# Where the last weights of a two-matrix feed-forward layer are converted: during attention, or beside the second pass

## The chip, the core and the metric

One NeuronCore of a Trainium2 chip runs the whole program in one launch. The metric is device time in microseconds (us), the median of several executions. PE is TensorE (matmul), DVE is VectorE, ACT is ScalarE, POOL is GpSimd, and SP is the engine whose queue issues nearly all DMA transfers here. Every engine executes its own instructions strictly in the order in which the build left them, and waits at an instruction until what it needs has happened.

## The reference, cut to what matters

```python
# q, k, v: (8 batches, 8 heads, 576 positions, 64)
scores = scale * q @ k.T                      # causal in blocks of 64 positions
attn = softmax(where(block_i >= block_j, scores, -1e9))
x = (attn @ v).transpose(0, 2, 1, 3).reshape(4608, 512)
out = ((x @ w_a) * (x @ w_b)) @ w_out         # w_a, w_b: 512 x 1536, w_out: 1536 x 512
```

The three weight matrices reach the kernel as 64-bit floating-point numbers, so they have to be turned into 32-bit numbers on the chip before TensorE can use them. This conversion is what the case is about.

## The kernel before, in words

**Blocks.** The 1536 hidden columns are 12 blocks of 128, numbered f = 0 to 11. A block needs its part of w_a and w_b (tensor `wab`, in two halves i = 0, 1 of 512 values a partition) and its rows of w_out (tensor `wo`, one piece of 512 values a partition). Every matmul is made of three: the operands are split into a high part that TensorE takes exactly (type fp32r) and a low rest, and high x high, high x low and low x high are added.

**Conversion of one piece** (`fetch`, `convert`, `sums`, `split`; L122 to L178). A DMA brings 512 KB into `raww`. Then come: DVE L139 (exponent out of the upper word, `sw`), ACT L140 (scaled exponent), DVE L143 and L145 (mantissa, `mw`), DVE L147 (sign and exponent together, `sw`) and DVE L149 (the 32-bit number, `xw`). A piece of `wo` is then split: ACT L110 writes the high part, DVE or POOL L113 the low one. A half of `wab` of the blocks 4 to 11 needs seven combinations instead of four (see the second pass): four small DVE sums (L172), two copies on ACT (L165, L175) and two subtractions on DVE (L177, L178). `convert` and `sums` are generators: each `next` is one step, and the steps are put between other work. With `paced`, a step's DVE instruction may not stand ahead of a named earlier instruction (`behind_of`).

**Attention** (64 heads, a slot of the loop at L598 for each). In a slot TensorE makes scores of one head (`sl`, `s`, L394, L414), turns the softmax result of the head before (`tp`, L467) and multiplies earlier ones with v (`av`, L516 to L522). DVE finds maxima (`nm`, L400), sums and the reciprocal of the sums (`rc`, L434 to L441); ACT makes exponentials (L403); POOL multiplies them by `rc` (`e`, L444); TensorE turns `e`; ACT copies it out of PSUM as high part (`ah`, L469) and DVE subtracts the low part (`al`, L471). Every second slot DVE also splits q of a pair of heads (`qp`, L341). SP copies q and k within the chip (`q<-qp`, `k<-kp`, L360, L361) two slots ahead of their use, through single buffers.

**First pass.** During attention the blocks 0 to 3 are applied to the tokens that are done (`ab_unit`, `o_unit`, `mm3`, L217), a fixed share of matmuls in each slot, and fill TensorE. Partial results go to DRAM (`part`). The product of a and b is `hf` (DVE, L243). The weights of these four blocks are converted in the first slots.

**Second pass** (L797 to L851). It covers six tiles of 768 tokens with the blocks 4 to 7 (`ps_` = 0), then the same six tiles with the blocks 8 to 11 (`ps_` = 1). For each block `pair_unit` makes seven products instead of eight (`psy`, `psx`, `psw`, `psv`, L705) that DVE combines (`u_z`, L723 to L733); POOL and ACT split the results (`h_z`), and `pair_out` (`pso_z`, L751) adds the four blocks. x is read back from DRAM (`xr`), and DVE, ACT and POOL form and split its combinations for the next tile (`sums_x`, L668).

**Where the blocks 4 to 11 are converted before the change.** The eight `wab` halves of the blocks 4 to 7 are converted while the first pass ends; their four `wo` pieces in the first tile. The weights of the blocks 8 to 11 (eight `wab` halves, four `wo` pieces) are converted during the tiles 1 to 4, one step for every 10 matmuls (`STEP2` = 1600), into a buffer `st`, and stored in DRAM (`wabd`, `wod`). In tile 5 they are loaded for the second sweep. The order of instructions within an engine is set at the build by a scheduler, in whose program order the steps stand where `next` is called.

## Time and profile before

| what | us |
|---|---|
| median of three runs (lowest, highest) | 1290.13 (1284.51, 1292.95) |
| the profiled execution, its own time | 1293.99 |
| its span, first to last instruction | 1292.2 |
| PE busy, share of the span | 1242.7, 96% |
| DVE busy, share of the span | 1000.4, 77% |
| ACT busy, share of the span | 686.9, 53% |
| POOL busy, share of the span | 545.0, 42% |

In a table of stretches each row gives the stretch, its length, then the busy time and number of instructions of PE, PEld (weight loads), DVE, ACT and POOL, the granted TensorE clock as a share of full speed, the busy share of the DMA engines and their GB/s. A stretch in which PE is busy for its whole length can get shorter only by fewer matmuls; where PE has idle time, the question is on whom it waited.

### The profile page before, as it was taken

Reading aid. Unit: us, or ns where it says so; the run is one execution under the profiler, and the core shown is the slowest. Engines: PE = TensorE matmul, PEld = TensorE weight load, DVE = VectorE, ACT = ScalarE, POOL = GpSimd, SP = SyncE. Lnnn points to the kernel's source line nnn. Section 1 sums busy time; section 2 is a strip of 40 time slices with the busy share of each in tenths; the row PEclk is TensorE's granted clock in tenths of the full one; section 3 lists DMA queues with packets and bytes.
Section 4 is the critical chain, followed back from the end, with each engine's and each line's share of the span. In section 5 each row is a group of like instructions: output and inputs, shape, how many; then the busy total and the mean of one; then the engine's idle time right before and its main releaser. Section 6 shows DMA issues by size and latency. Waiting matters only on the chain.

```text
span 1292.2 us, 23401 instructions
## 1 busy us (share of the span) xinstructions
PE 1242.7 (96%) x7849; PEld 1177.4 (91%) x7849; DVE 1000.4 (77%) x2325; ACT 686.9 (53%) x1722; POOL 545.0 (42%) x681
## 2 busy tenths in 40 slices
PE   9998999999999999999998998999999899999998
PEld 5677989999999999999997998999999899999998
DVE  6877778778878787887789999899976576577563
ACT  5787777788787887887745423233322222222210
POOL 4667555555565555655522223223123123123231
PEclk8999999999999999999998999999999899999999
DMA  5466667766676666677224355464466442242131
GB/s 194 138 188 169 170 170 180 176 166 171 165 182 171 168 178 164 163 187 172 82 93 149 111 190 163 163 195 157 159 205 238 160 148 65 83 147 87 61 98 62
DMA packets 93496, 196.58 MB, mean 152 GB/s; under 512 B 11968, under 2 KB 52928, under 8 KB 93376
## 3 DMA queue, kind: packets, MB, share of 16 engines
q1 hardware_dynamic: 88768, 185.64, 50.8%
q10 hardware_dynamic: 4608, 9.44, 2.0%
q8 instruction: 63, 1.03, 0.3%
q14 instruction: 57, 0.47, 0.1%
HBM read 96.47 MB, written 47.19 MB: 111 GB/s over the span
## 4 chain that ended last, share of the span: by engine, by line
PE 61%; DVE 21%; issue 6%; DMA 5%; ACT 4%; POOL 2%; SPq 0%; ACTq 0%; DVEq 0%; POOLq 0%
PE pso_z L751 13%; PE ps L217 8%; PE psx_z L705 6%; PE psw_z L705 6%; PE psv_z L705 6%; PE tp L467 5%; DVE al L471 3%; PE s L394 3%; PE pso L217 3%; DVE nm L400 3%; PE psy_z L705 3%; PE av L522 2%; PE av L506 2%; POOL e L444 2%; DMA kp<-kT 1%
## 5 line engine op out<-in xcount | busy, mean ns | idle before, releaser
L113 POOL TENSOR_TENSOR h_z<-u_z,h_z 128x384 fp32r<-128x384 f32 x96 | 112.9, 1176 | 400.8 <-ACT h_z L110 378.2
L217 PE MATMUL ps<-xh,wab 128*128 128x288 f32 x1024 | 245.9, 306 | 0.0
L444 POOL TENSOR_SCALAR e<-e,rc 128x512 f32<-128x512 f32 (+3 forms) x256 | 152.3, 608 | 154.6 <-DVE rc L441 148.1
L751 PE MATMUL pso_z<-h_z,wo 128*128 128x384 f32 x1152 | 203.8, 335 | 3.5 <-POOL h_z L113 3.5
L751 PEld LDWEIGHTS pso_z<-h_z,wo 128*128 128x128 f32 x1152 | 199.6, 188 | 5.8 <-POOL h_z L113 5.8
L471 DVE TENSOR_TENSOR al<-tp,ah 128x512 fp32r<-128x512 f32 x224 | 138.8, 620 | 63.7 <-ACT ah L469 61.6
L217 PEld LDWEIGHTS ps<-xh,wab 128*128 128x128 f32 x1024 | 173.7, 190 | 3.6
L467 PE MATMUL tp<-ident,e 128*128 128x128 f32 x832 | 136.3, 279 | 18.5 <-POOL e L444 11.6
L217 PE MATMUL ps<-xl,wab 128*128 128x288 f32 x512 | 152.8, 299 | 0.2 <-POOL xl L113 0.2
L110 ACT CAST h_z<-u_z 128x384 fp32r<-128x384 f32 x96 | 49.4, 514 | 167.2 <-DVE u_z L730 162.1
L469 ACT CAST ah<-tp 128x512 fp32r<-128x512 f32 x224 | 119.2, 534 | 35.0 <-PE tp L467 33.3
L467 PEld LDWEIGHTS tp<-ident,e 128*128 128x128 f32 x832 | 99.3, 142 | 36.2 <-POOL e L444 21.4
L217 PE MATMUL pso<-hh,wo 128*128 128x288 f32 x512 | 128.5, 312 | 3.2 <-ACT hh L110 3.2
L705 PE MATMUL psx_z<-xh,wab 128*128 128x384 f32 x384 | 118.5, 344 | 9.0 <-DVE u_z L723 8.6
L403 ACT ACTIVATE e<-s,nm 128x192 f32<-128x192 f32 (+2 forms) x192 | 101.8, 531 | 36.7 <-DVE nm L400 30.1
L705 PE MATMUL psw_z<-xh,wab 128*128 128x384 f32 x384 | 117.3, 341 | 0.8 <-DVE u_z L725 0.8
L705 PE MATMUL psv_z<-xh,wab 128*128 128x384 f32 x384 | 117.2, 340 | 0.5 <-DVE u_z L727 0.4
L400 DVE TENSOR_REDUCE nm<-s 128x1 f32<-128x128 f32 (+3 forms) x256 | 110.2, 432 | 4.4
L217 PEld LDWEIGHTS ps<-xl,wab 128*128 128x128 f32 x512 | 97.3, 190 | 3.9 <-POOL xl L113 0.4
L217 PEld LDWEIGHTS pso<-hh,wo 128*128 128x128 f32 x512 | 89.2, 193 | 5.3 <-ACT hh L110 3.9
L113 POOL TENSOR_TENSOR v<-vr,v 128x320 fp32r<-128x320 f32 x56 | 49.4, 883 | 85.6 <-ACT v L110 63.7
L394 PE MATMUL s<-k,q 128*128 128x256 f32 x336 | 81.7, 325 | 2.6 <-ACT e L403 1.4
(143 smaller groups left out, 2913.3 us busy)
## 6 DMA issues: line engine op xcount, KB each, us to landing
k<-kp SPq DMA_DIRECT2D x112, 288.0 KB, 4.0
xr<-xd SPq DMA_DIRECT2D x48, 384.0 KB, 3.5
pt<-part SPq DMA_DIRECT2D x96, 192.0 KB, 3.5
q<-qp SPq DMA_DIRECT2D x112, 160.0 KB, 2.8
raww<-wab SPq DMA_DIRECT2D x24, 512.0 KB, 3.8
qp<-qT SPq DMA_DIRECT2D x32, 320.0 KB, 3.1
vr<-vm SPq DMA_DIRECT2D x64, 160.0 KB, 3.4
kp<-kT SPq DMA_DIRECT2D x32, 288.0 KB, 3.1
```

The source lines that it names most:

```text
L110: nc.scalar.copy(hi, src)
L113: return lo_eng.tensor_tensor(lo, src, f32(hi), op=ALU.subtract)
L217: mm = nc.tensor.matmul(ps, w_, d_, start=(i == 0), stop=(i == n - 1))
L394: mark = nc.tensor.matmul(ps[:, :w], qm[:, q0[t]:q0[t] + P], kk[:, :w], start=(i == 0), stop=(i == len(ks) - 1))
L400: nc.vector.tensor_reduce(nm[:, t:t + 1], view, axis=AX.X, op=ALU.max, negate=True)
L403: nc.scalar.activation(out, view, AF.Exp, bias=bias, accum_out=sm[:, t, :1])
L444: nc.gpsimd.tensor_scalar(ev, ev, rc[:, t:t + 1], 1.0, op0=ALU.mult, op1=ALU.mult)
L467: mark = nc.tensor.transpose(tp[:, c], src, ident)
L469: nc.scalar.copy(ah[:, :m, cols], tp[:, :m])
L471: return nc.vector.tensor_tensor(al[:, :m, cols], tp[:, :m], f32(ah[:, :m, cols]), op=ALU.subtract)
L705: nc.tensor.matmul(ps, wt[:, i, iw], j[:, ix], start=start and kp == 0 and i == 0 and j is xh, stop=kp == KP - 1 and i == 1, skip_group_ch ...
L751: nc.tensor.matmul(ps, wt[:, a, osl], b, start=i == 0, stop=i == 3 * len(fs) - 1)
```

## The change

All eight `wo` pieces of the blocks 4 to 11 and the four `wab` halves of the blocks 8 and 9 are now converted during attention, from slot 13 on, by a new generator `convert_to_dram`. It has no `st` buffer: the high part goes into a buffer of the ring that `raww` uses (two buffers), the low part overwrites `xw` and `mw`, and each is stored in DRAM by a DMA of its own on SP's queue. 76 steps are spread evenly over the slots 13 to 63, at two places of a slot (`k` = 6 and 9), each DVE instruction behind the last `rc`. The low parts, on POOL or DVE before, are DVE's. `wo` of the blocks 4 to 7 is loaded from DRAM when the second pass begins. The blocks 10 and 11 (four `wab` halves) stay in the second pass and go one step to some 19 matmuls (`STEP2` = 3000).

```diff
-STEP2 = 1600
+STEP2 = 3000
...
-    wod = dram.tile([F2, P, 2 * DO], F32, name="wod")
+    wod = dram.tile([2 * F2, P, 2 * DO], F32, name="wod")
...
+    def convert_to_dram(todo, paced):
+
+        for f, i in todo:
+            raw = fetch(wab[f, :, i] if i < KP else wo[f], f"w{f}_{i}")
+            yield
+            xf, spare = yield from convert(raw, f"w{f}_{i}", paced)
+            n = f"st{f}_{i}"
+            hi = wpool.tile([P, 2 * NO, P], F32R, tag="raw", name=n, bufs=2)
+            if i == KP:
+                hi = hi[:, :NO].rearrange("p c n -> p (c n)")
+                lo = xf.bitcast(F32R)
+                split(hi, lo, xf, nc.scalar, nc.vector)
+                nc.sync.dma_start(wod[f - F1, :, :DO], f32(hi))
+                nc.sync.dma_start(wod[f - F1, :, DO:], f32(lo))
+            else:
+                hi = hi[:, :NW]
+                lo = yield from sums(hi, None, xf, spare, paced)
+                to = wabd[f - F1 - F2, i]
+                nc.sync.dma_start(to[:, :NW * P], f32(hi).rearrange("p c n -> p (c n)"))
+                nc.sync.dma_start(to[:, NW * P:][:, :3 * P], f32(lo[0]).rearrange("p c n -> p (c n)"))
+                nc.sync.dma_start(to[:, (NW + 3) * P:], f32(lo[1]).rearrange("p c n -> p (c n)"))
+            yield
...
+    HALF = F1 + F2 + F2 // 2
+    later = convert_to_dram(parts(range(F1, NF), [KP]) + parts(range(F1 + F2, HALF), range(KP)), "rc")
+    LATER_FROM, LATER_STEPS = 13, 2 * F2 * 6 + F2 // 2 * KP * 7
...
+            while k in (6, 9) and n_later < LATER_STEPS * (now - LATER_FROM) / (NH - 1 - LATER_FROM):
+                next(later, None)
+                n_later += 1
...
-    conv = convert_w(parts(range(F1, F1 + F2)), nc.vector, paced=True)
+    conv = convert_w(parts(range(F1, F1 + F2), range(KP)), nc.vector, paced="hf")
...
-    stage = pool(left, "stage", 1, reuse_waits="tile")
...
+    for f in range(F1, F1 + F2):
+        load_wo(f)
...
-                conv = convert_w(parts(range(F1 + F2, NF)), nc.vector, paced=True, stage=stage)
+                conv = convert_to_dram(parts(range(HALF, NF), range(KP)), "hf")
```

Where the build put the moved instructions is seen at three places. The first is DVE in attention, from the reciprocal `rc` of one slot to the next head's first `al`; `s` and `nm` belong to the scores of the head after. Before:

```order
L441 RECIPROCAL rc_1_4740<-rc_1_4740 128x5
L429 MEMSET s_2_4947 64x64
L400 TENSOR_REDUCE nm_2_4900<-s_2_4947 128x1
L429 MEMSET s_2_4904 64x64
L400 TENSOR_REDUCE nm_2_4900<-s_2_4904 128x1
L471 TENSOR_TENSOR al_1_4982<-tp_1_3_4983,ah_1_4981 128x4x128
L527 TENSOR_TENSOR xf_0_4957<-av_0_4994,avlo_0_5001 64x64
```

The same place now, where the line numbers of the changed file are some 21 higher:

```order
L462 RECIPROCAL rc_1_4822<-rc_1_4822 128x5
L450 MEMSET s_2_5034 64x64
L143 TENSOR_SCALAR mw_2_4913<-raww_2_4802 128x512
L421 TENSOR_REDUCE nm_2_4987<-s_2_5034 128x1
L450 MEMSET s_2_4991 64x64
L145 SCALAR_TENSOR_TENSOR mw_2_4913<-raww_2_4802,mw_2_4913 128x512
L421 TENSOR_REDUCE nm_2_4987<-s_2_4991 128x1
L492 TENSOR_TENSOR al_1_5069<-tp_1_3_5070,ah_1_5068 128x4x128
L548 TENSOR_TENSOR xf_0_5044<-av_0_5082,avlo_0_5089 64x64
```

Two conversion instructions stand between the reciprocal and the two maxima. At the same place the slot before this one has `sw` (L139), the slot after it the second `sw` (L147), and the next one `xw` (L149) ahead of the first maximum and the low part (L113) ahead of `al`: a piece of `wo` takes four slots. The slots with `sw` are those in which `qp` follows before the next reciprocal. The second place is ACT in a slot with `sw`; `e` are exponentials, `ah` is the copy that `al` waits for. Now:

```order
L424 ACTIVATE e_3_123,sm_127<-sl_1_4824,nb_1_4823 128x512
L140 ACTIVATE sw_2_4912<-sw_2_4912,shift 128x512
L424 ACTIVATE e_0_120,sm_127<-s_1_4864,nm_1_4821 128x192
L110 CAST hh_1_2_4888<-hf_1_2_4886 128x288
L490 CAST ah_0_4903<-tp_0_3_4905 128x4x128
L424 ACTIVATE e_1_121,sm_127<-s_1_4825,nm_1_4821 128x320
```

The row with `sw` is new and stands ahead of `e` and `ah`; the other rows stand in this sequence before, too. In the slots without `hf` at this place, `ah` has moved ahead of the second `e`. The third place is DVE in the second pass's first tile, from the first `u_z` of block 4 on. Before:

```order
L723 TENSOR_TENSOR u_z_0_4_10567<-psx_z_0_4_10500,u_z_0_4_10567 128x384
L149 TENSOR_TENSOR xw_2_10508<-mw_2_10507,sw_2_10506 128x512
L725 TENSOR_TENSOR u_z_0_4_10568<-psw_z_0_4_10501,u_z_0_4_10567 128x384
L139 TENSOR_SCALAR sw_2_10520<-raww_2_10504 128x512
L113 TENSOR_TENSOR wo_10515<-xw_2_10508,wo_10515 128x512
L143 TENSOR_SCALAR mw_2_10521<-raww_2_10504 128x512
L147 SCALAR_TENSOR_TENSOR sw_2_10520<-raww_2_10504,sw_2_10520 128x512
L145 SCALAR_TENSOR_TENSOR mw_2_10521<-raww_2_10504,mw_2_10521 128x512
L727 TENSOR_TENSOR u_z_0_4_10568<-psv_z_0_4_10502,u_z_0_4_10568 128x384
```

Now:

```order
L708 TENSOR_TENSOR xt_1_0_10938<-xr_1_10789,xr_1_10787 128x384
L709 TENSOR_TENSOR xr_1_10787<-xr_1_10787 128x384
L710 TENSOR_TENSOR xt_1_0_10938<-xr_1_10789,xr_1_10787 128x384
L757 TENSOR_TENSOR u_z_0_4_10754<-psx_z_0_4_10723,u_z_0_4_10754 128x384
L713 TENSOR_TENSOR xt_1_0_10938<-xr_1_10789,xt_1_0_10938 128x384
L759 TENSOR_TENSOR u_z_0_4_10755<-psw_z_0_4_10724,u_z_0_4_10754 128x384
L761 TENSOR_TENSOR u_z_0_4_10755<-psv_z_0_4_10725,u_z_0_4_10755 128x384
L763 TENSOR_TENSOR u_z_0_4_10756<-psw_z_0_4_10724,u_z_0_4_10754 128x384
```

No conversion is left between the `u_z`, and the combinations of x for the next tile (`xt`, `xr`) have moved up to them. Counted from the first `u_z` of a tile to that of the next, DVE has 30, 23, 29, 26 and 16 rows of conversion in the tiles 0 to 4 before, and 2, 12, 16, 10 and 0 now.

More of the change, by code (lines that the diff above doesn't have):

```diff
@@ L135, in step @@
             if paced:
-                behind_of(ins, "hf")
+                behind_of(ins, paced)
         step(v.tensor_scalar(s, hi, 20, 0x7FF, op0=ALU.logical_shift_right, op1=ALU.bitwise_and))
@@ L153, in attention_then_bilinear_ffn, with parts @@
     w_sb = {}
-    def parts(fs):
-        return [(f, i) for f in fs for i in range(KP)] + [(f, KP) for f in fs]
+    def parts(fs, which=range(KP + 1)):
+        return [(f, i) for f in fs for i in which if i < KP] + [(f, i) for f in fs for i in which if i == KP]
     def new_wo(f):
@@ L173, in sums, with convert_w @@
         if paced:
-            behind_of(ins, "hf")
+            behind_of(ins, paced)
         nc.scalar.copy(hi[:, 3:], t)
         yield
-        v.tensor_tensor(lo[:, :3], x[:, 1:], f32(hi[:, :3]), op=ALU.subtract)
-        v.tensor_tensor(lo[:, 3:], t, f32(hi[:, 3:]), op=ALU.subtract)
-    def convert_w(todo, lo_eng, paced=False, stage=None):
+        if lo is None:
+            lo = x[:, 1:].bitcast(F32R), t.bitcast(F32R)
+        else:
+            lo = lo[:, :3], lo[:, 3:]
+        v.tensor_tensor(lo[0], x[:, 1:], f32(hi[:, :3]), op=ALU.subtract)
+        v.tensor_tensor(lo[1], t, f32(hi[:, 3:]), op=ALU.subtract)
+        return lo
+    def convert_w(todo, lo_eng, paced=None):
         def ahead(f, i):
@@ L188, in convert_w @@
             xf, spare = yield from convert(now, f"w{f}_{i}", paced)
-            if stage:
-                st = stage.tile([P, 2, NW if i < KP else NO, P], F32R, tag="st", name=f"st{f}_{i}")
             if i == KP:
-                if not stage and w_sb[f][1] is None:
-                    new_wo(f)
-                o = st.rearrange("p j c n -> p j (c n)") if stage else w_sb[f][1]
+                o = w_sb[f][1]
                 split(o[:, 0], o[:, 1], xf, nc.scalar, lo_eng)
@@ L200, in convert_w @@
             else:
-                ab = st if stage else w_sb[f][0][:, i]
+                ab = w_sb[f][0][:, i]
                 yield from sums(ab[:, 0], ab[:, 1], xf, spare, paced)
-            if stage:
-                f -= F1 + F2
-                nc.sync.dma_start(wod[f] if i == KP else wabd[f, i], f32(st).rearrange("p j c n -> p (j c n)"))
+            yield
[12 more added lines that the diff above has]
+                nc.sync.dma_start(wod[f - F1, :, DO:], f32(lo))
+            else:
+                hi = hi[:, :NW]
[4 more added lines that the diff above has]
+                nc.sync.dma_start(to[:, (NW + 3) * P:], f32(lo[1]).rearrange("p c n -> p (c n)"))
             yield
@@ L576, in attention_then_bilinear_ffn @@
     conv = convert_w(parts(range(F1)), nc.gpsimd)
-    n_moe = n_conv = 0
+    HALF = F1 + F2 + F2 // 2
+    later = convert_to_dram(parts(range(F1, NF), [KP]) + parts(range(F1 + F2, HALF), range(KP)), "rc")
+    LATER_FROM, LATER_STEPS = 13, 2 * F2 * 6 + F2 // 2 * KP * 7
+    n_moe = n_conv = n_later = 0
     for p in range(2):
@@ L636, in attention_then_bilinear_ffn @@
                 n_moe += 1
+    for _ in later:
+        pass
     order.close()
@@ L654, in attention_then_bilinear_ffn, with load_wo @@
     upool = pool(right, "upool", 2, "right", reuse_waits="tile")
+    def load_wo(f):
+        new_wo(f)
+        nc.sync.dma_start(f32(w_sb[f][1]).rearrange("p j n -> p (j n)"), wod[f - F1])
     def new_w(f):
@@ L833, in attention_then_bilinear_ffn @@
                 if ps_ == 0 and tt == NT2 - 1:
+                    background(1e4)
                     new_w(f + F2)
@@ L847, in attention_then_bilinear_ffn @@
             if ps_ == 0 and tt == NT2 - 1:
-                background(1e4)
                 for f in fs:
-                    new_wo(f + F2)
-                    nc.sync.dma_start(f32(w_sb[f + F2][1]).rearrange("p j n -> p (j n)"), wod[f - F1])
+                    load_wo(f + F2)
     left.close()
```

## The prediction

> **What bounds the kernel now.** I cut the span into stretches first: attention from slot 13 on, the end of the first pass, and the twelve tiles of the second pass, from the first `psy` of each.
>
> ```profile
> 131.86:629.68 497.82, 484.15 (x3476) 463.96 (x3476) 391.00 (x1176) 393.98 (x1096) 284.39 (x424) 1.00 0.66 167
> 640.00:709.36 69.36, 62.89 (x435) 60.65 (x435) 62.39 (x129) 34.82 (x75) 17.75 (x19) 0.95 0.42 134
> 709.36:757.72 48.36, 47.40 (x266) 45.78 (x265) 47.90 (x81) 19.46 (x33) 16.16 (x12) 1.00 0.46 143
> 757.72:810.76 53.04, 47.86 (x265) 45.75 (x265) 48.98 (x86) 17.64 (x30) 13.53 (x10) 1.00 0.53 175
> 810.76:859.38 48.62, 47.41 (x265) 45.62 (x265) 43.71 (x76) 15.55 (x27) 13.56 (x10) 1.00 0.48 160
> 859.38:908.29 48.91, 47.42 (x266) 45.79 (x265) 46.49 (x81) 17.07 (x29) 13.47 (x10) 1.00 0.54 185
> 908.29:956.72 48.43, 47.60 (x265) 45.73 (x265) 45.32 (x71) 15.30 (x26) 13.44 (x10) 1.00 0.46 153
> 956.72:1003.17 46.45, 46.45 (x265) 46.28 (x265) 27.72 (x44) 9.19 (x17) 13.15 (x10) 1.00 0.70 247
> 1003.17:1056.33 53.16, 48.93 (x266) 48.45 (x265) 35.30 (x58) 13.45 (x23) 13.17 (x10) 0.94 0.43 142
> 1056.33:1102.80 46.47, 46.47 (x265) 46.30 (x265) 31.37 (x51) 11.37 (x20) 13.14 (x10) 1.00 0.34 101
> ```
>
> TensorE bounds everything: a tile without conversions (the rows from 956.72 and 1056.33) takes 46.45 us with PE busy throughout. The tiles 0 to 4, which carry conversions, are 1.9, 6.6, 2.2, 2.5 and 2.0 us longer, 15.2 us together, and DVE is busy for 90 to 99% of them. The 6.7 us of the second sweep's first tile (the row from 1003.17) are no conversion's. In attention PE idles 13.7 of 497.8 us, and DVE 106.8.
>
> Second I asked on whom PE waited: the largest wait in attention (us in total, times, longest), and the largest single stall among the tiles, in tile 1.
>
> ```profile
> PE tp L467 <- POOL e L444: 9.7, 24, 0.8
> ```
>
> ```profile
> 797.30 0.97 PE L751 MATMUL pso_z<-h_z,wo 128*128 128x384 f32 x4 [2.57 <-POOL h_z L113]
> ```
>
> In attention it is the first turned tile of a head that is late: `rc` on DVE, then POOL's `e`, then `tp`. DVE is thus near the bound in both places, and the change takes its work from one to the other.
>
> **What is taken out of the second pass.** Tile 0 loses its four `wo` pieces, and the tiles 1 to 4, which had twelve pieces, keep four. The conversion rows on DVE fall from 30, 23, 29, 26, 16 to 2, 12, 16, 10, 0 by the order. If a tile's excess followed its rows, 15.2 us would become 0.1 + 3.4 + 1.2 + 1.0 + 0 = 5.7. I take 4.7: tile 1 also inherits late x combinations from tile 0, and in the order these have moved up among the first `u_z`. That is **-10.5 us**. The bounds: -15.2, all of it, and -4, if tile 1 keeps its 6.6 for its DMAs and a half stays elsewhere. `wo` of the blocks 4 to 7 is still 512 KB a piece on SP, now from `wod`: nothing. The eight `wab` halves converted before 709.36, where PE idles 6.5 us, stay: nothing. The loads ahead of the row 1003.17 stay: nothing.
>
> **What is put into attention.** DVE's share of a piece is read from the first slots, where conversions already run beside attention, and from the second pass for what only `wab` of the later blocks has:
>
> ```profile
> L145 DVE SCALAR_TENSOR_TENSOR mw<-raww,mw 128x512 f32<-128x512 uint16 x12 | 10.8, 901 | 0.2
> L149 DVE TENSOR_TENSOR xw<-mw,sw 128x512 f32<-128x512 f32 x12 | 9.9, 828 | 0.3
> L147 DVE SCALAR_TENSOR_TENSOR sw<-raww,sw 128x512 int32<-128x512 int32 x12 | 9.7, 809 | 3.1 <-ACT sw L140 3.1
> L143 DVE TENSOR_SCALAR mw<-raww 128x512 int32<-128x512 int32 x12 | 7.1, 596 | 0.0
> L139 DVE TENSOR_SCALAR sw<-raww 128x512 int32<-128x512 int32 x12 | 5.7, 476 | 0.1
> L113 DVE TENSOR_TENSOR wo<-xw,wo 128x512 fp32r<-128x512 f32 x4 | 2.8, 708 | 0.0
> L172 DVE TENSOR_TENSOR mw<-xw 128x128 f32<-128x128 f32 x32 | 9.0, 320 | 0.2
> L178 DVE TENSOR_TENSOR st<-mw,st 128x512 fp32r<-128x512 f32 x8 | 5.8, 725 | 0.2 <-ACT st L175 0.2
> L177 DVE TENSOR_TENSOR st<-xw,st 128x384 fp32r<-128x384 f32 x8 | 4.4, 546 | 0.0
> ```
>
> A `wo` piece: 0.90 + 0.83 + 0.81 + 0.60 + 0.48 + 0.71 = 4.33 us; a `wab` half: 3.62 + 4 x 0.32 + 0.73 + 0.55 = 6.18 us. Eight and four of them: 34.6 + 24.7 = **59 us** on DVE in 50 slots, 1.2 us a slot, against 2.1 us of idle time a slot. By the sum it fits; but the engine is in order, and what counts is where its idle time lies. ACT gets 28 instructions more (a scaled exponent and one or two copies a piece). SP gets 12 loads and 28 stores; a store waits for its low part, and behind it on SP stand `q` and `k` copies.
>
> ```profile
> k<-kp SPq DMA_DIRECT2D x112, 288.0 KB, 4.0
> ```
>
> I cost the stores at nothing, since those copies are for two slots later; without that cover each of the 12 pieces would make one copy late by its 4.0 us to landing, 48 us.
>
> What a microsecond on DVE costs here can be read twice. Two pairs of slots follow each other with equal matmuls, and the second has two more `hf`. The first rows are all engines, the next `hf` alone:
>
> ```profile
> 551.49:571.19 19.70, 19.35 (x142) 18.63 (x141) 15.45 (x46) 15.80 (x44) 10.55 (x16) 1.00 0.72 187
> 571.19:591.00 19.81, 19.31 (x142) 18.60 (x141) 16.07 (x48) 15.77 (x44) 12.12 (x18) 1.00 0.64 158
> ```
>
> ```profile
> 551.49:571.19 19.70, 0.46 (x1) 1.00 0.72 187
> 571.19:591.00 19.81, 1.35 (x3) 1.00 0.64 158
> ```
>
> 0.89 us more `hf` lengthen the pair by 0.11 us, an eighth. The other reading is the slot with the last piece converted so far and the slot behind it:
>
> ```profile
> 99.18:109.61 10.43, 9.95 (x66) 8.59 (x65) 10.19 (x28) 8.54 (x24) 8.83 (x11) 1.00 0.53 173
> 109.61:119.03 9.42, 8.67 (x59) 7.91 (x59) 7.41 (x26) 7.44 (x22) 5.69 (x10) 1.00 0.77 174
> ```
>
> Five conversion instructions (3.6 us by the means above) go with 1.01 us more, a bit over a quarter, though the two slots differ in first-pass work too. So 59 us cost between 7 and 17 us; I take a quarter, as the nearer case is the one with conversions: **+15 us**. The bounds are 0 (nothing in attention is removed, so no gain) and 47: all 59 less the 12.0 us for which DVE waits on PE itself, in this row:
>
> ```profile
> DVE s L415 <- PE s L414: 12.0, 24, 0.6
> ```
>
> **The sum.** The profiled execution took 1293.99 us, its span 1292.2: 1293.99 - 10.5 + 15 = 1298.5. It lies 3.9 us above the median shown, so the median should go from 1290.13 to about **1295 us**, 0.4% up. A measurement of this kernel can tell about 1%, 13 us, from no change.
>
> **A rule that speaks against the change.** POOL's `e` runs directly behind the reciprocal, and there the new DVE instructions stand too. Beside the early conversions and then without them it took:
>
> ```profile
> L444 POOL TENSOR_SCALAR e<-e,rc x40: 420/692/1719, 16.0 to 106.3; 128x512 f32<-128x512 f32 x10, 128x448 f32<-128x448 f32 x10, 128x320 f32<-128x320 f32 x10, 128x192 f32<-128x192 f32 x10
> L444 POOL TENSOR_SCALAR e<-e,rc x160: 424/592/701, 207.3 to 595.8; 128x512 f32<-128x512 f32 x40, 128x448 f32<-128x448 f32 x40, 128x320 f32<-128x320 f32 x40, 128x192 f32<-128x192 f32 x40
> ```
>
> The longest `e` grows from 0.70 to 1.72 us. The Trainium skill ("SBUF — State Buffer", section "Who interferes with whom") says that a DVE instruction with two SBUF inputs, or in a mode that uses both ports, and a POOL instruction that reads SBUF exclude each other for a whole instruction. These rows agree with it. By the rule alone the first new instruction of each slot waits for an `e`; with the 0.59 us median of an `e`, 50 slots give an estimate of 30 us, the time of the second rival below.
>
> **The rivals.**
>
> *Attention takes it all in.* For it: DVE's 106.8 idle us, the eighth of the `hf` pair, and `ah` that moved ahead of the second `e`, which shortens what DVE waits for. Against it: the slot at 99.18. With +0 it gives 1290.1 - 10.5 = 1279.6; with the whole 15.2 us it would be 1275.
>
> *The turn behind the reciprocal decides; slower than before.* Here is one slot's DVE, from a reciprocal on:
>
> ```profile
> 564.05 0.18 DVE L441 RECIPROCAL rc<-rc 128x5 f32<-128x5 f32 x1
> 564.46 0.36 DVE L400 TENSOR_REDUCE nm<-s 128x1 f32<-128x192 f32 x1
> 566.62 0.69 DVE L471 TENSOR_TENSOR al<-tp,ah 128x512 fp32r<-128x512 f32 x1 [1.16 <-ACT ah L469]
> 570.72 0.11 DVE L415 MEMSET s<- 64x64 f32 x1 [0.53 <-PE s L414]
> ```
>
> The one large gap, 1.16 us ahead of `al`, waits for ACT's `ah`. A new instruction ahead of `nm` delays the exponential, and with it `ah` behind it: the gap moves along instead of filling. Only the 0.53 us ahead of L415 are free, and in the slots with `qp` there is no such gap at all, so there a delay goes through `rc` and `e` to `tp`. Half the slots, half of the 59 us: +30, and 1290.1 + 30 - 10.5 = 1310. It decides once a slot's new work is over 0.5 us, which three of the four slots of a piece exceed. Against it stands the `hf` pair.
>
> *The second pass hardly gets shorter.* Tile 1's stall of 2.57 us hangs on POOL's `h_z`, and its DMA share of 0.53 is high among the tiles; if DVE is not what makes these tiles long, the gain is the lower bound: 1290.1 + 15 - 4 = 1301. Against it: tile 5, with the highest DMA share (0.70) and no conversion, has no excess.
>
> **How the numbers follow.** The forecast (1283 to 1303) gets 0.42, absorbed 0.20, the turn 0.28, little gain 0.10. The range goes from 1279, attention free, to 1318, the turn with some of its bound. Faster by over 1% (below 1277) needs nearly all of the 15.2 us with a free attention: 0.09. Slower by over 1% (above 1303): most of the turn, half of the little gain, a little of the forecast: 0.34. The same: 0.57.
>
> **What would show it.** The tiles 0 to 4 should take 46.5 to 50 us, tile 4 46.45, tile 1 under 50. The fifty slots from 13 on should take about 513 us instead of 498, with DVE busy near 450, and `tp` waiting for `e` for about 20 us instead of 9.7. The prediction is wrong if the slots stay within 3 us of 498 (then the DVE price failed), if they grow by 25 or more (then it was the turn), or if tile 1 stays above 52 (then its excess was not DVE's).

## The result, and the profile after

The changed kernel takes 1302.87 us (median of six runs, 1300.03 to 1307.24), the one before beside it 1290.24 us: a ratio of 1.010, 95% interval 1.0075 to 1.0131. It is about 1% slower, 8 us above the forecast of 1295. The profiled execution of the changed kernel took 1300.03 us, its lowest; that of before was 1293.99, above the highest of its timed executions (1292.95). So the two traces differ by 6 us only, and are compared by stretches. The stretches of the changed kernel are the same as in the prediction: the 50 slots from 13 on, the end of the first pass, the six tiles of the first sweep, and the first tile of the second.

```profile
126.23:649.90 523.67, 492.73 (x3474) 463.39 (x3474) 431.26 (x1269) 407.44 (x1125) 315.36 (x425) 1.00 0.71 188
649.90:730.58 80.68, 74.40 (x511) 71.71 (x510) 71.32 (x150) 42.83 (x98) 24.16 (x28) 0.94 0.37 120
730.58:776.71 46.13, 46.13 (x266) 45.98 (x265) 35.55 (x59) 15.18 (x26) 14.20 (x11) 1.00 0.43 139
776.71:823.73 47.02, 46.78 (x265) 45.80 (x265) 38.91 (x63) 13.16 (x23) 13.25 (x10) 1.00 0.42 135
823.73:870.48 46.75, 46.65 (x265) 46.00 (x265) 38.71 (x66) 14.00 (x26) 13.77 (x10) 1.00 0.40 125
870.48:917.23 46.75, 46.47 (x266) 45.67 (x265) 40.65 (x67) 13.50 (x24) 13.84 (x10) 1.00 0.48 159
917.23:963.70 46.47, 46.47 (x265) 46.30 (x265) 31.35 (x51) 11.38 (x20) 13.13 (x10) 1.00 0.34 99
963.70:1010.16 46.46, 46.46 (x265) 46.30 (x265) 27.62 (x44) 9.18 (x17) 13.12 (x10) 1.00 0.71 249
1010.16:1062.34 52.18, 48.26 (x265) 47.76 (x265) 35.38 (x59) 13.45 (x23) 13.12 (x10) 0.97 0.44 144
```

The fifty slots grew from 497.82 to 523.67 us, by 25.9 instead of 15. POOL, which got no instruction, is busy for 315.4 us in them instead of 284.4. The tiles of the first sweep and the first of the second lost 48.36 + 53.04 + 48.62 + 48.91 + 48.43 + 46.45 + 53.16 - 331.76 = 15.2 us instead of 10.5. Of this 14.2 us lie in the tiles 0 to 4, the ones that the change relieves. The other 1.0 is the second sweep's first tile, which has no conversion and takes from 49.4 to 53.8 us in the profiles of this case. The rest of the difference of the two traces is the first 13 slots, which the change does not touch (131.86 us before, 126.23 now), and 1 us at the end of the first pass. The wait that the prediction named doubled as forecast:

```profile
PE tp L488 <- POOL e L465: 20.1, 37, 1.2
```

It was 9.7 us in 24 waits. What remains to be explained is 11 us too much in attention, and 5 us too much gain in the second pass.

### The profile page after: what moved, and what is told of

It reads as the page before. It is cut to its first block, busy times and chain, and to the rows that moved or that the text cites. A ratio compares the mean times of both kernels' runs of the same rounds, so it can differ in the third digit from the quotient of the medians.

```text
span 1298.2 us, 23437 instructions
## 1 busy us (share of the span) xinstructions
PE 1244.1 (96%) x7849; PEld 1176.3 (91%) x7849; DVE 995.1 (77%) x2325; ACT 682.1 (53%) x1722; POOL 574.4 (44%) x681
## 4 chain that ended last, share of the span: by engine, by line
PE 58%; DVE 19%; ACT 7%; DMA 6%; issue 5%; POOL 5%; SPq 1%; ACTq 0%; DVEq 0%; POOLq 0%
PE pso_z L785 14%; PE psx_z L739 7%; PE psw_z L739 7%; PE psv_z L739 7%; PE tp L488 5%; DVE al L492 4%; PE ps L238 4%; POOL e L465 4%; PE psy_z L739 4%; DVE nm L421 3%; PE pso L238 2%; PE s L415 2%; ACT ah L490 2%; DMA q<-qp 2%; PE av L543 2%
## 5 line engine op out<-in xcount | busy, mean ns | idle before, releaser
L113 POOL TENSOR_TENSOR h_z<-u_z,h_z 128x384 fp32r<-128x384 f32 x96 | 112.3, 1170 | 395.3 <-ACT h_z L110 383.1
L465 POOL TENSOR_SCALAR e<-e,rc 128x512 f32<-128x512 f32 (+3 forms) x256 | 176.6, 700 | 134.8 <-DVE rc L462 127.9
L110 ACT CAST h_z<-u_z 128x384 fp32r<-128x384 f32 x96 | 49.4, 515 | 195.2 <-DVE u_z L764 193.8
L113 POOL TENSOR_TENSOR hl<-hf,hh 128x288 fp32r<-128x288 f32 x64 | 54.2, 847 | 69.1 <-ACT hh L110 67.2
```

The costliest lines, as they stand in the source:

```text
L110: nc.scalar.copy(hi, src)
L113: return lo_eng.tensor_tensor(lo, src, f32(hi), op=ALU.subtract)
L465: nc.gpsimd.tensor_scalar(ev, ev, rc[:, t:t + 1], 1.0, op0=ALU.mult, op1=ALU.mult)
```

## The experiments

**How they are read.** A slot runs from the start of one head's first maximum (`nm<-sl`) to the next head's. The build leaves attention's own order nearly alone, and equal slots mostly come out equal to 0.03 us in different kernels, so the slots 13 to 62 of two kernels can be subtracted one by one. A kernel with no conversion in them (`none`, the first experiment) is the zero. The column in the middle takes the thirty slots 23 to 52, away from the first collisions of slot 14 and from the end. Before, with the same attention as `none`, shows the noise: four slots differ by 0.7 to 1.1 us, the others by less than 0.4, most by 0.03 or less. Each row is one profiled execution. In `none`, `dma_only`, `no_dma`, `reduce`, `reduce_no_dma`, `no_act` and `dve_only` the second pass loads attention output in the place of the pieces; these were executed once, `none` four times, the full kernels four to ten times. The diffs are cut to the lines that matter. Where an experiment has a generator of its own, its lines stand against those of `convert_to_dram`; those of `reduce_no_dma` against `reduce`, and those of `dve_only` against `no_act`.

| kernel | what of the 12 pieces is in attention | 50 slots, us | above `none` | of it slots 23 to 52 |
|---|---|---|---|---|
| `none` | nothing | 496.5 | 0 | 0 |
| before | nothing | 497.8 | 1.3 | 1.2 |
| `dma_only` | DMA, in the slots 14 to 30 | 506.3 | 9.8 | 7.1 |
| `reduce_no_dma` | DVE time of another kind, ACT | 505.7 | 9.3 | 1.9 |
| `no_dma` | DVE, ACT | 511.0 | 14.6 | 8.8 |
| `dve_only` | DVE | 513.0 | 16.5 | 9.1 |
| `reduce` | DVE time of another kind, ACT, DMA | 513.0 | 16.5 | 6.7 |
| `no_act` | DVE, DMA | 513.2 | 16.7 | 10.7 |
| changed | all | 523.7 | 27.2 | 14.5 |
| `split_b` | all, raw loads elsewhere | 526.8 | 30.3 | 17.0 |
| `gap` | all, steps behind the second maximum | 514.5 | 18.0 | 6.9 |
| `gap_all` | as `gap`, loose steps tied too | 506.2 | 9.7 | 4.7 |
| `wo_only` | the 8 `wo` pieces | 508.5 | 12.0 | 10.5 |
| `gap_wo` | the 8 `wo` pieces, as `gap` | 501.3 | 4.8 | 5.1 |

**1. `none`: no conversion in attention, the second pass as changed.**

```diff
-            while k in (6, 9) and n_later < LATER_STEPS * (now - LATER_FROM) / (NH - 1 - LATER_FROM):
-                next(later, None)
-                n_later += 1
...
-        nc.sync.dma_start(f32(w_sb[f][1]).rearrange("p j n -> p (j n)"), wod[f - F1])
+        nc.sync.dma_start(f32(w_sb[f][1]).rearrange("p j n -> p (j n)"), xd[:P, :2 * DO])
```

> Leaves out the twelve conversions of the attention part; the second pass loads attention output in the place of those pieces, so its values are not the reference's. Everything else is the changed kernel, and attention has the instruction order of before. All theories of attention's cost (DVE's queue, the port shared with POOL, DMA traffic, ACT's copies) expect the 50 slots back at about 498 us (before 497.8, changed 523.7). It measures the gain of the second pass by itself: if the 15 us of the trace are real, the time is about 1275 us, a ratio of 0.988 to before; if the gain was the 10.5 us forecast, 1280 us, 0.992.

Measured: 1276.65 us against 1290.60 of before beside it, ratio 0.989 (0.985 to 0.993), that is 14.0 us; the slots:

```profile
130.56:627.03 496.47, 483.56 (x3476) 463.68 (x3476) 390.83 (x1175) 393.71 (x1096) 285.00 (x424) 1.00 0.66 168
```

The gain of the second pass is real, and by the trace it is 13 to 15 us: the seven tiles took 332.1 us here, 14.9 less than before, and the six of the first sweep 13.1 less. The timed runs alone would allow 9 to 20 us. Nearly everything else is attention's.

**2. `dma_only`: loads and stores without arithmetic.**

```diff
+            bits = raw.rearrange("p n w -> p (n w)")
+            to = spare_d[f - F1]
...
+                nc.sync.dma_start(to[:, :DO], bits[:, :DO])
+                nc.sync.dma_start(to[:, DO:2 * DO], bits[:, DO:])
```

> Leaves out all arithmetic of the twelve pieces in attention: each piece is loaded and as many bytes are stored from the loaded tile by as many DMAs; the second pass loads attention output in their place. If DMA traffic or SP's queue of issues costs the slots their time, the 50 slots stay at 518 to 524 us. If it is the work on DVE and ACT, they are at 498 to 502 us.

```profile
128.66:634.97 506.31, 486.29 (x3475) 463.51 (x3474) 389.22 (x1177) 393.88 (x1097) 286.01 (x424) 1.00 0.73 191
```

506.3 us is neither answer. It is also a weak experiment: with nothing to wait for, the build put all twelve pieces into the slots 14 to 30, where 8.4 of the 9.8 us lie. It shows that the transfers can cost on their own, not what they cost in the changed kernel's places.

**3. `no_dma`: the work without the transfers.**

```diff
-            raw = fetch(wab[f, :, i] if i < KP else wo[f], f"w{f}_{i}")
+        raw = fetch(wo[F1], "w_one")
...
-                nc.sync.dma_start(wod[f - F1, :, :DO], f32(hi))
-                nc.sync.dma_start(wod[f - F1, :, DO:], f32(lo))
```

> Keeps every DVE and ACT instruction of the twelve pieces in attention, on one raw tile that is loaded once, and leaves out the other loads and all stores; the second pass loads attention output in their place. If it is the work on DVE and ACT, the 50 slots stay at 518 to 524 us and POOL's e at a mean near 700 ns. If it is DMA traffic or SP's queue, they are at 498 to 505 us.

```profile
131.06:642.10 511.04, 488.17 (x3473) 461.43 (x3474) 429.45 (x1269) 405.73 (x1125) 314.60 (x424) 1.00 0.66 165
```

Between the answers again: 14.6 us above `none`, 12.6 under the changed kernel. Without the DMAs the instructions cost just the 15 us of the prediction, and the DMAs, costed at nothing, add almost as much here. POOL is busy for 30 us more than in `none` (314.6), with no transfer and no instruction of its own added.

**4. `reduce`: other instructions of the same length on DVE.**

```diff
+            def red(a):
+                ins = nc.vector.tensor_reduce(m[:, :1], a, axis=AX.X, op=ALU.max)
+                behind_of(ins, paced)
+
+            red(src[:, :264])
+            nc.scalar.activation(s, src, AF.Relu, bias=m[:, :1])
```

> In the twelve pieces in attention each DVE instruction is replaced by a tensor_reduce of about the same duration at the same place; ACT's work, loads and stores stay in number and size, the values are not the conversion's, and the second pass loads attention output in their place. If DVE's time in the queue is what costs, whatever the instruction, the 50 slots stay at 518 to 524 us. If it is the exclusion of DVE and POOL (instructions with two inputs in SBUF against POOL's e), which a reduce with one input does not take part in, they are at 500 to 508 us, and POOL's e is back from a mean of 700 to about 610 ns.

**5. `reduce_no_dma`: the same without loads and stores.**

```diff
-            raw = fetch(wab[f, :, i] if i < KP else wo[f], f"w{f}_{i}")
+        raw = fetch(wo[F1], "w_one")
...
-                nc.sync.dma_start(to[:, :DO], hi_i[:, :DO])
-                nc.sync.dma_start(to[:, DO:2 * DO], s_i)
```

> Leaves out the conversion's values, its loads and its stores: in attention each DVE instruction of the twelve pieces is a tensor_reduce of about the same duration, ACT's 28 instructions stay, nothing is loaded (but once) or stored; the second pass loads attention output in their place. It is the place in the queues of DVE and ACT alone. If the three costs add (queues 6 to 7, DMA 10, the exclusion of DVE and POOL 10 to 11 us, by the four runs before), the 50 slots take 501 to 505 us and POOL's busy time in them is 285 us. If the exclusion does not exist and the reduces were only kinder in combination with the DMAs, the slots take 509 to 513 us as with the true instructions without DMA.

The two kernels' slots, one after the other:

```profile
126.30:639.32 513.02, 488.88 (x3475) 464.55 (x3475) 422.66 (x1268) 409.12 (x1126) 285.93 (x425) 0.99 0.73 192
```

```profile
126.99:632.73 505.74, 487.57 (x3475) 464.98 (x3474) 421.42 (x1269) 408.12 (x1125) 286.06 (x424) 0.99 0.66 167
```

`reduce` lies between its two answers, `reduce_no_dma` just above the sum of 501 to 505, far from the 509 to 513 of the other. POOL is back at 286 us, and each pair differs by the kind of DVE instruction: 10.7 us with DMAs (523.7 to 513.0), 5.3 without (511.0 to 505.7). The reduces are 45.6 us of DVE against 55.2 in `no_dma`, so a part of that is plain time; but in the thirty slots in the middle the reduces cost only 1.9 us and the true instructions 8.8. There DVE's queue has room, and what costs is the meeting with POOL. Two differences remain. In the `wab` halves every reduce is tied behind the reciprocal, while three of the four true sums and both differences are loose; in the slots 23 to 42, which hold `wo` pieces alone, it is 1.0 against 5.6 us. And a reduce writes one value a partition where the true instruction writes 512, so it is not shown whether the meeting is over reading or over writing. POOL's groups of `e`, `no_dma` first, then `reduce_no_dma`:

```profile
L478 POOL TENSOR_SCALAR e<-e,rc 128x512 f32<-128x512 f32 x200 | 139.2, 707 | 109.4 <-DVE rc L475 109.4
```

```profile
L503 POOL TENSOR_SCALAR e<-e,rc 128x512 f32<-128x512 f32 x200 | 114.6, 588 | 109.0 <-DVE rc L500 108.0 <-DMA vr<-vm 0.8
```

On average an `e` takes 707 ns in `no_dma`, 588 with reduces at the same place, and 582 in `none`. One slot shows it whole. Slot 39, from the reciprocal on, in `none`, in the changed kernel, and in `reduce_no_dma`: the step on DVE, POOL's first two `e`, the next maximum `nm`, and TensorE's first `tp`. The slot begins at 389.17, 400.63 and 390.15.

```profile
391.55 0.18 DVE L462 RECIPROCAL rc<-rc 128x5 f32<-128x5 f32 x1
391.82 1.32 POOL L465 TENSOR_SCALAR e<-e,rc 128x512 f32<-128x512 f32 x2 [3.90 <-DVE rc L462]
...
391.95 0.36 DVE L421 TENSOR_REDUCE nm<-s 128x1 f32<-128x192 f32 x1
...
392.68 0.60 PE L488 MATMUL tp<-ident,e 128*128 128x128 f32 x4
```

```profile
403.01 0.18 DVE L462 RECIPROCAL rc<-rc 128x5 f32<-128x5 f32 x1
403.29 1.84 POOL L465 TENSOR_SCALAR e<-e,rc 128x512 f32<-128x512 f32 x2 [3.90 <-DVE rc L462]
403.30 0.67 DVE L147 SCALAR_TENSOR_TENSOR sw<-raww,sw 128x512 int32<-128x512 int32 x1
...
403.89 0.34 DVE L421 TENSOR_REDUCE nm<-s 128x1 f32<-128x192 f32 x1
...
404.57 0.66 PE L488 MATMUL tp<-ident,e 128*128 128x128 f32 x4 [0.27 <-POOL e L465]
```

```profile
392.80 1.31 POOL L503 TENSOR_SCALAR e<-e,rc 128x512 f32<-128x512 f32 x2 [3.90 <-DVE rc L500]
392.81 0.62 DVE L218 TENSOR_REDUCE m<-raww_one 128x1 f32<-128x512 f32 x1
393.36 0.34 DVE L459 TENSOR_REDUCE nm<-s 128x1 f32<-128x192 f32 x1
...
393.66 0.60 PE L526 MATMUL tp<-ident,e 128*128 128x128 f32 x4
```

In all three the reciprocal stands 2.38 us into the slot. With the conversion's step behind it, the two `e` take 1.84 us instead of 1.32, `tp` starts 3.94 us into the slot instead of 3.51 and waits 0.27 us for `e`, and the slot takes 10.05 us instead of 9.58. The reduce of 0.62 us at the same place costs nothing: 9.57. Yet it holds up the next maximum nearly as long: `nm` starts 3.21 us into the slot, 3.26 in the changed kernel and 2.78 in `none`. So in this slot the late maximum is free, and the late `e` is not. The Trainium skill ("SBUF — State Buffer", section "Who interferes with whom") says that a DVE instruction with two inputs in SBUF excludes a POOL instruction that reads SBUF, and that a reduce on trn2 never takes part; the three fences agree with both. It also says that whoever issues first keeps the other out. That these rows don't show: POOL's `e` is listed 0.01 us ahead of the step, and it is the one that gets longer.

**6. `no_act`: ACT's part left out.**

```diff
-        nc.scalar.activation(s, s, AF.Relu, scale=2.0 ** 23, bias=shift)
+        if act:
+            nc.scalar.activation(s, s, AF.Relu, scale=2.0 ** 23, bias=shift)
...
-                split(hi, lo, xf, nc.scalar, nc.vector)
+                nc.vector.tensor_tensor(xf, xf, spare, op=ALU.subtract)
```

> Leaves out ACT's 28 instructions of the twelve pieces in attention (the exponent's relu, the copies of the high parts); DVE's instructions, loads and stores stay in number, size and operands in SBUF, the values are not the conversion's, and the second pass loads attention output in their place. If ACT's queue is a good part of the cost, the 50 slots come down to 510 to 515 us. If the cost is DVE with POOL, and the DMAs, they stay at 518 to 524 us with POOL busy near 314 us.

**7. `dve_only`: neither ACT's part nor DMAs.** As `no_act`, and:

```diff
-            raw = fetch(wab[f, :, i] if i < KP else wo[f], f"w{f}_{i}")
+        raw = fetch(wo[F1], "w_one")
...
-                nc.sync.dma_start(to[:, :DO], hi[:, :DO])
-                nc.sync.dma_start(to[:, DO:2 * DO], xf.bitcast(I32))
```

> Leaves out loads, stores and ACT's part of the twelve pieces in attention; only DVE's instructions stay, on one loaded tile, behind the reciprocal as in the changed kernel; the values are not the conversion's and the second pass loads attention output in their place. If the costs simply add (ACT 10.5 by the run without its instructions, DMA 12.6 by the run without DMAs, of 27.2 us), little is left: 498 to 503 us in the 50 slots. If ACT and DMA cost in the same slots, where either alone is taken in, the two removals overlap and the slots stay at 508 to 512 us.

The slots of `no_act`, then of `dve_only`:

```profile
127.32:640.48 513.16, 488.85 (x3476) 461.65 (x3475) 432.27 (x1269) 393.83 (x1098) 314.42 (x424) 1.00 0.72 190
```

```profile
130.06:643.07 513.01, 489.69 (x3476) 463.91 (x3476) 429.59 (x1268) 393.48 (x1096) 314.41 (x424) 1.00 0.65 163
```

The removals overlap: `dve_only` is at 513.0, a little above the 508 to 512 stated for that, and nowhere near 498 to 503. By its expectation `no_act` speaks for ACT as the price, and that reading is wrong. `dve_only` differs from `no_dma` by ACT's instructions alone, and it is not shorter (513.0 against 511.0). So ACT's part costs nothing that these runs show. `no_act` had changed a second thing: with no high part to write, its buffer ring holds raw tiles only, and the next raw load goes out a slot earlier. That points at the moment of the loads: in `no_act` all loads and stores together add 0.2 us to the slots (513.2 against 513.0 of `dve_only`; 1.6 us in the thirty in the middle). Slot 45 is read in the changed kernel (it begins at 461.88), SP first, then ACT and DVE:

```profile
455.75 0.56 SPq L124 DMA_DIRECT2D raww<-wab  x1
456.40 0.42 SPq L218 DMA_DIRECT2D wod<-st  x1
456.92 0.38 SPq L219 DMA_DIRECT2D wod<-xw  x1
458.71 0.47 SPq L381 DMA_DIRECT2D q<-qp  x1
...
465.85 0.34 SPq L346 DMA_DIRECT2D qp<-qT  x1
```

```profile
468.88 0.74 ACT L361 ACTIVATE qp<-qp 128x640 fp32r<-128x640 f32 x1 [1.15 <-DMA qp<-qT]
469.65 0.83 DVE L362 SCALAR_TENSOR_TENSOR qp<-qp 128x640 f32<-128x640 f32 x1 [1.44 <-ACT qp L361]
```

And in `no_dma`, where the slot begins at 456.59:

```profile
453.45 0.47 SPq L394 DMA_DIRECT2D q<-qp  x1
...
458.30 0.33 SPq L359 DMA_DIRECT2D qp<-qT  x1
```

```profile
463.11 0.82 DVE L375 SCALAR_TENSOR_TENSOR qp<-qp 128x640 f32<-128x640 f32 x1 [0.19 <-ACT qp L374]
```

The first copy of q is issued 3.2 us ahead of the slot in both. In the changed kernel a load and two stores, 1 MB together, went out on the same queue 1.8 to 3.0 us before it. The two copies of q then take longer from issue to landing (the median of the two in us, last in the row), first in the changed kernel, then in `no_dma`:

```profile
q<-qp SPq DMA_DIRECT2D x2, 160.0 KB, 5.7
```

```profile
q<-qp SPq DMA_DIRECT2D x2, 160.0 KB, 3.0
```

The next load of qT has to wait until these copies have landed, because `qp` has a single buffer: it is issued 4.0 us into the slot instead of 1.7, ACT's scaling waits 1.15 us for it, DVE's 1.44 instead of 0.19, and the slot is 1.24 us longer. The same late load, issued 3.1 to 4.0 us into the slot, and a wait of DVE's `qp` of 0.64 to 1.44 us stand in the slots 25, 29, 33, 37, 41 and 45, which hold 5.0 of the 12.6 us between the two kernels. In `no_act`, where the load goes out a slot earlier, qT is issued 1.4 to 2.1 us into these slots and `qp` waits 0.2 us. Slot 27 has the wait (0.80 us) without a late qT. Slot 18 waits 1.48 us on DVE for its own raw load. The slots 14, 20 to 22 and 54, with most of the rest, were not traced further.

**8. `split_b`: the raw load moved away from the copies.**

```diff
+        if after:
+            behind_of(ins, after)
...
-            raw = fetch(wab[f, :, i] if i < KP else wo[f], f"w{f}_{i}")
+            raw = fetch(wab[f, :, i] if i < KP else wo[f], f"w{f}_{i}", "qT" if paced == "rc" else None)
```

> A full kernel: the changed one, but each raw load of a piece in attention is tied behind the last qT load on SP's queue, so that it no longer stands with the two stores of the piece before (1 MB in all) directly ahead of two heads' copies of q and k. Nothing else is moved by hand. In the slots 33 to 45 of the changed kernel the next qT load was issued about 2 us later than with the load elsewhere, ACT's scaling of q waited 0.3 to 1.2 us for it, and DVE's as long again. If this late qT is what the DMAs cost, the 50 slots come down from 523.7 to 511 to 517 us (DVE's work alone took 513.0), and the time to 1287 to 1293 us. If it is ACT's 28 instructions, or the traffic as such, they stay at 520 to 526 us.

Measured: 1311.2 us, ratio 1.015 (1.010 to 1.020), 526.8 us in the slots. The expectation fell. In the slots 33 and 37 the wait of DVE's `qp` went to 0.19 us and the slot to 0.3 and 0.4 above `none` (1.0 and 0.7 in the changed kernel), but others got longer. Behind the qT load the raw load stands ahead of the next kT, on which POOL's split of k hangs, and what SP waits for k is the larger for it. The changed kernel, then `split_b`:

```profile
SPq L382 <- POOL kp L368: 49.1, 24, 4.7
```

```profile
SPq L384 <- POOL kp L370: 70.2, 24, 9.8
```

So the late qT is one way in which the DMAs cost, and the load's place alone isn't the cure.

**9. `gap`: the steps behind the second maximum.** All twelve pieces and all DMAs; DVE's steps now stand where DVE waits for `ah`, not directly behind the reciprocal.

```diff
+            ins = top(t, ps[:, :nk[t]])
+            if t == 1:
+                last["nm"] = ins
...
-    later = convert_to_dram(parts(range(F1, NF), [KP]) + parts(range(F1 + F2, HALF), range(KP)), "rc")
+    later = convert_to_dram(parts(range(F1, NF), [KP]) + parts(range(F1 + F2, HALF), range(KP)), "nm")
```

> A full kernel: the conversion's steps in attention stand behind the second maximum of the slot instead of directly behind the reciprocal, ahead of the lowering that waits for ACT. If the place behind the reciprocal is what costs (the theory of the prediction), the 50 slots come down from 523.7 to 508 to 515 us and the time to 1285 to 1292 us. If POOL's exclusion and the DMAs are what costs, the steps still fall on POOL's scaling of e, POOL stays busy for 314 us or more in the slots, and they take 519 to 526 us, the time 1298 to 1306 us.

Measured: 1289.33 us, ratio 0.998 (0.996 to 1.001).

```profile
124.40:638.88 514.48, 492.29 (x3473) 467.21 (x3474) 436.50 (x1268) 405.75 (x1124) 313.40 (x424) 0.99 0.72 191
```

Both theories were half right: slots and time came down as the place would have it, and POOL stayed as busy as the exclusion would have it (313.4). Slot 39 (it begins at 388.24) shows how these go together:

```profile
390.89 1.31 POOL L467 TENSOR_SCALAR e<-e,rc 128x512 f32<-128x512 f32 x2 [3.89 <-DVE rc L464]
...
391.75 0.60 PE L490 MATMUL tp<-ident,e 128*128 128x128 f32 x4
...
392.18 0.88 POOL L467 TENSOR_SCALAR e_s<-e_s,rc 128x128 f32<-128x128 f32 x1
392.22 0.68 DVE L147 SCALAR_TENSOR_TENSOR sw<-raww,sw 128x512 int32<-128x512 int32 x1
```

The step now meets `e_s`, which takes 0.88 us instead of 0.37. TensorE turns `e_s` later; the first `tp` starts 3.51 us into the slot as without a conversion, and the slot takes 9.58 us as in `none`. The exclusion is paid by a POOL instruction for which nobody waits. The slots 23 to 42 together cost 0.6 us, with all DMAs. 13 of the 18 us lie in the slots from 43 on, nearly all of them those of the `wab` halves.

The edit changed a second thing. In slot 45 (it begins at 447.51) the next qT load is as late as in the changed kernel, 4.3 us into the slot, but the build has put DVE's `qp` behind the next maximum, where it waits for nothing:

```profile
451.80 0.34 SPq L346 DMA_DIRECT2D qp<-qT  x1
```

```profile
455.38 0.62 DVE L421 TENSOR_REDUCE nm<-s 128x1 f32<-128x448 f32 x1
455.92 0.81 DVE L362 SCALAR_TENSOR_TENSOR qp<-qp 128x640 f32<-128x640 f32 x1
```

The order is the same in the slots 25, 29, 33, 37 and 41. These six slots cost 6.4 us in the changed kernel and nothing here, so much of the 9.2 us between the two kernels is the late qT, taken in by this order, and not the exclusion.

**10. `gap_all`: the loose steps of the halves tied as well.** In `sums` only the fourth sum was tied to a place. A half now has nine steps instead of seven, so all pieces are spread anew over the slots.

```diff
             ins = v.tensor_tensor(t[:, d], a, b, op=op)
+            if paced == "nm":
+                behind_of(ins, paced)
+                if d == 1:
+                    yield
```

> A full kernel: all twelve pieces in attention behind the second maximum, and now the sums and the last two differences of the w_a, w_b halves too, two sums or one difference a slot, where before only the fourth sum was tied to a place. In the run without these ties slots 43 to 62 took 13 of the 18 us. If those loose instructions of 0.3 to 0.7 us cost them, the 50 slots come down from 514.5 to 501 to 507 us and the time to 1278 to 1284 us. If it is the halves' three stores and 960 KB, or ACT's two copies, they stay at 511 to 515 us.

Measured: 1283.31 us, ratio 0.995 (0.993 to 0.997), and 506.2 us in the slots, as expected of the loose steps; from slot 43 on 1.3 us are left of the 13. But the slots 23 to 42, whose `wo` steps stand behind the second maximum as in `gap`, cost 5.6 us again instead of 0.6; the slots 29, 33, 37 and 41 take 1.1 to 1.8 us more each. So the place alone does not make them free; what else it takes was not tested.

```profile
127.19:633.37 506.18, 486.43 (x3473) 463.20 (x3474) 436.30 (x1268) 407.66 (x1124) 312.77 (x424) 1.00 0.73 194
```

**11. `wo_only`: eight pieces instead of twelve, behind the reciprocal.**

```diff
-    HALF = F1 + F2 + F2 // 2
+    HALF = F1 + F2
-    LATER_FROM, LATER_STEPS = 13, 2 * F2 * 6 + F2 // 2 * KP * 7
+    LATER_FROM, LATER_STEPS = 13, 2 * F2 * 6
...
-STEP2 = 3000
+STEP2 = 1500
```

> A full kernel: only the eight pieces of w_out are converted during attention, and the eight halves of w_a, w_b of blocks 8 to 11 in the first sweep of the second pass. Of 56 us of DVE work 36 are left in attention, of 37 DMAs 24. If the cost is proportional to the work moved, the 50 slots take 497 + 26 x 0.64 = 514 us, and the sweep gives back some 2 to 5 us of its gain: 1293 to 1300 us in all, a ratio of 1.003 to 1.008 to before. If the last four pieces cost more than their share (their stores stand at the end of attention), it comes to 1288 to 1293 us.

Measured: 1289.77 us, ratio 1.000 (0.997 to 1.003). The slots come to 508.5 us, less than in proportion, and the seven tiles to 334.4, so 12.5 us of the gain stay; 3.6 of these lie in the second sweep's first tile, and 9.0 in the first sweep.

```profile
124.83:633.32 508.49, 486.39 (x3473) 461.63 (x3474) 411.49 (x1225) 402.72 (x1112) 307.00 (x424) 1.00 0.69 182
```

**12. `gap_wo`: the edits of 9 and 11 together.**

```diff
-    later = convert_to_dram(parts(range(F1, NF), [KP]) + parts(range(F1 + F2, HALF), range(KP)), "rc")
+    later = convert_to_dram(parts(range(F1, NF), [KP]) + parts(range(F1 + F2, HALF), range(KP)), "nm")
...
-    HALF = F1 + F2 + F2 // 2
+    HALF = F1 + F2
```

> A full kernel: only the eight pieces of w_out in attention, their steps behind the second maximum of the slot; the eight halves of w_a, w_b of blocks 8 to 11 in the first sweep. In the run with all twelve pieces at that place the slots of the w_out pieces (13 to 42) took 5 us more than without conversions, of that 6 in two slots at the start. If the place decides (DVE's instruction meets POOL's scaling behind the one that the transposes wait for), the 50 slots take 498 to 503 us, the sweep gains 12 us over before as with the eight pieces alone, and the time is 1279 to 1284 us, a ratio of 0.990 to 0.995. If the place only looked better by chance of the instruction order, the slots take 506 to 510 us as with the eight pieces behind the reciprocal, and the time is 1287 to 1291 us.

Measured: 1282.84 us, ratio 0.995 (0.993 to 0.997), 501.3 us in the slots. The seven tiles kept 10.4 us of gain, 8.6 of it in the first sweep.

```profile
125.65:626.96 501.31, 485.69 (x3474) 462.07 (x3474) 419.87 (x1225) 402.29 (x1113) 303.04 (x425) 1.00 0.70 184
```

`gap_wo` and `gap_all` beat both kernels, by 0.5% the one before and by about 1.5% the changed one, each compared through the kernel before beside it; the two cannot be told apart.

## Why the prediction was right, and where it was wrong

The direction was right: the likeliest case was a small loss that is hard to tell from no change, and 1302.87 lies in the range and just inside the forecast's own (1283 to 1303). But two terms of the sum were wrong, with opposite signs: attention cost 25.9 us instead of 15, and the second pass gave 15.2 instead of 10.5. That the total missed by only 8 us is partly luck, because the second error took nearly half of the first away. And attention grew by more than the 25 us at which the prediction itself calls its account of it wrong.

*The second pass, -10.5.* Mis-sized: 15.2 us in the trace, 14.2 of it in the tiles 0 to 4, which the term is about, and 14.0 by the timed runs of `none`. The failed step is "if a tile's excess followed its rows". The tiles 1 to 3 kept 12, 16 and 10 rows of conversion and were to keep 3.4, 1.2 and 1.0 us with them, less 1.0 in all; they are only 0.6, 0.3 and 0.3 above 46.45. DVE is busy for 83 to 87% of them now, and for 90 to 95% before: what still fits costs next to nothing. The true value lay close to the bound of -15.2. Tile 4 came out as stated (46.47), and tile 1 with 47.02 is well under 50, so the third rival is out.

*Attention, +15.* The price of DVE's own work, a quarter of 59 us, was right: 14.6 us (`no_dma`) and 16.5 (`dve_only`). This is partly luck too: the quarter was read from one pair of slots that could not tell two causes apart, and the runs show both. The failed step is "I cost the stores at nothing, since those copies are for two slots later". The cover is there for the copies, but not for what stands behind them: the next qT load waits in a single buffer until they have landed, and about one slot after the copies ACT and DVE wait for it. The transfers came to some 11 to 13 us on top, about 1 us in each of a dozen slots; 5.0 us in six slots are traced to qT, 1.6 in slot 18 to its raw load, and the rest is open. It is no fixed price of the transfers: they add 7.3 us beside reduces and 0.2 us without ACT's part. The 48 us that the prediction gave for a failed cover (4.0 us for each piece) was the right question with too high a price: in slot 45 qT went out 2.3 us later, and the slot is 1.24 us longer.

*What makes the 15 us.* The prediction named two causes without deciding: DVE's turn behind the reciprocal, and the exclusion with POOL. Both work at the same place. In the thirty middle slots it is mostly the exclusion: 8.8 us with the true instructions, 1.9 with reduces. At both ends the place in the queues of DVE and ACT costs as well, without any load or store (7.4 of the 9.3 us of `reduce_no_dma`); why there was not taken apart. So over all fifty slots the exclusion is the smaller part of the 14.6 us by these two runs (5.3).

*The second rival.* Its number for attention (30) was closer than mine, and by the prediction's own sign (25 us or more) it would be the one. Its place was right as far as moving the steps took 9 of the 27 us away, and 17 with all of them tied, though the moves also changed where `qp` stands. Its mechanism was mostly wrong: it let the work itself delay `nm`, `ah` and `al`, half of 59 us, and the reduces show that this delay is nearly free in the middle slots, 9.3 us in all. The estimate from the Trainium skill's rule, 30 us for the exclusion, was too high for the same slots: 5 to 11 us were seen.

*The signs.* `tp` waiting for `e`: 20 us stated, 20.1 measured. DVE busy near 450 us in the slots: wrong, 431. The new rows add up to 56 us, but neighbouring rows of DVE overlap by up to 0.1 us each in the trace, 11.5 us more in all than in `none`, and attention's own rows got 4.5 us shorter. So busy times of rows do not simply add.

## What to carry to other kernels

Work put into an engine's idle time can cost by whom it meets more than by its length: ask which POOL instruction runs at that moment and who waits for that one, and try the step beside one for which nobody waits. Then look at what else the build moved. A transfer is not hidden because its neighbours in the queue are early; follow the buffer that they free to the load behind it. And a stretch of equal, deterministic slots, subtracted slot by slot from a run without the work, tells 0.3 us apart in most slots where whole runs of one kernel differ by 7 to 15.

## What the runs showed of the hardware

- A reduce of 0.62 us on DVE from SBUF leaves a POOL scaling as it is (two `e` in 1.31 us); a two-input instruction of 0.67 us that starts within 0.01 us of it stretches it to 1.84 us and is itself not stretched. I had expected the new DVE instruction to wait. Elsewhere in the slots it does: the low part L113 takes a mean of 985 ns in the changed kernel, against 708 in the row of the prediction. In six slots it starts 0.29 us after an `e` and takes 0.88 us; in slot 20 it meets no POOL instruction and takes 0.69.

```profile
L113 DVE TENSOR_TENSOR xw<-xw,st 128x512 fp32r<-128x512 f32 x8 | 7.9, 985 | 0.5 <-ACT st L110 0.5
```

- A DVE instruction with one input in SBUF can stretch POOL as well. In the slots 25, 29, 33, 37, 41 and 45 of the changed kernel L139 takes 0.41 us, and the `e` beside it 0.97 us instead of 0.70.

- From the first instruction to slot 13 the fourteen profiles took from 124.4 to 131.9 us, though nothing was changed there: about as much as single runs of one kernel differ by.
